# Merging score jobs, pairing output evacuations and moving a weight load in a fused attention + MLP kernel

## The chip, the cores and the metric

The kernel runs on one core of one Trainium2 chip. The metric is the device time of one execution in microseconds. Profiles give a span that is some 2 us shorter than the timed execution.

## The reference

```python
def _attn_ref(q, k, v):                     # batch 8, heads 8, seq 576, head_dim 64, fp32
    scores = q @ k.transpose(0, 1, 3, 2) / np.sqrt(64)
    mask_local   = (rel >= 0) & (rel < 32)                              # heads 0..3
    mask_strided = (rel >= 0) & (pos[None, :] % 32 == pos[:, None] % 32)  # heads 4..7
    attn = softmax(where(mask, scores, -1e9))
    return attn @ v

def _moe_ref(x, w_in, w_out):               # x: 4608 tokens x 512, d_ff 2048
    h = x @ w_in
    return (h * tanh(softplus(h))) @ w_out  # mish
```

The kernel computes only the scores that the masks keep. A local head is 6 windows of 96 queries. A strided head is, per residue mod 8, a product of 72 by 72.

## The kernel before

The main loop goes over 9 blocks of 512 tokens. In block t, TensorE does the first MLP product (8 groups, each evacuated by a Mish on ScalarE) with the transposes of q and k of batch t+1 woven in, and then the second product (16 groups, output rows `ot` 0 to 3) with the attention of batch t+1 woven in by steps. Blocks 7 and 8 have no attention left. I call the two parts of a block its first and second half, and what comes before block 0 the prologue.

A score job is a few matmuls into one PSUM tile, one exp on ScalarE, and one multiplication with a mask on VectorE or GpSimd:

```python
def qk(self, kind, hp, hf, meng, from_mm=False):     # 8 jobs per batch
    ps = tile_s(from_mm); pt = P[self.n % NP]        # NP = 8 buffers of [128, 2, 352]
    ...                                              # 6 or 8 small matmuls
    nc.scalar.activation(pt[0:n, :, 0:288], ps[0:n, :, 0:288], AF.Exp, scale=scale)
    meng.tensor_tensor(out=pt[0:n, :, 0:288], in0=pt[0:n, :, 0:288], in1=<mask>, op=ALU.mult)
```

`pv(kind, i)` multiplies with v (four matmuls), then VectorE takes a reciprocal and a product. `xt(kind, hf)` transposes the result, and ScalarE copies it to `xT`, the input of the MLP. The output is copied out row by row of a two-row PSUM tile:

```python
p = po[ot // 2]                                      # [128, 2, 512] fp32: two banks
for fc in range(4 * g4, 4 * g4 + 4):
    nc.tensor.matmul(p[:, ot % 2, :], lhsT=gT[...], rhs=w_out[:, fc, :], ...)
if g4 == 3:
    osb = o_pool.tile([128, DM], F32, ...)
    nc.scalar.copy(osb[:], p[:, ot % 2, :])
    nc.sync.dma_start(out[r:r + 128, :], osb[:])
```

The steps of the attention beside the 16 groups, and the prologue's GpSimd order:

```python
[Q("s",0,0,Po)], [], [Q("s",1,0,Dv)], [Q("s",0,1,Po)], [Q("s",1,1,Dv), V("s",0)],
[Q("l",0,0,Po), V, V], [Q("l",1,0,Po), V], [Q("l",0,1,Po), V, V], [Q("l",1,1,Dv), V],
... [V("l",5)], [X("l",1)]

cast_qk_loc(0, Po, Dv)
load_w_in()                       # GpSimd queue, cast fp32 -> bf16 by the transfer
a.qk("s", 0, 0, Po) ...           # strided jobs, masks half on GpSimd
cast(Sc, vs ...)                  # on ScalarE
cast(Po, vl ...) x2               # on GpSimd: waits for v
...
a.qk("l", ..., Po) x4             # local masks all on GpSimd
load_qk_str(1); load w_out        # GpSimd queue
cast_qk_loc(1, Po, Po); cast_v(1, Po, Po); load_qk_str(2) ...
```

The softmax here doesn't subtract the row's maximum and nothing guards it: scores larger than these inputs give would overflow.

Of the kernel before, what the change touches and what calls it, by code (L numbers as in the profile page):

```python
# [10 lines left out]
F32 = mybir.dt.float32  # L11
BF16 = mybir.dt.bfloat16
AF = mybir.ActivationFunctionType
# [3 lines left out]
NW = 6  # L17
WQ = 96
CL, PL = 6, 96
CS, PN = 8, 72  # L20
# [3 lines left out]
def _masks():  # L24
    kk = np.arange(128)[:, None]
    qq = np.arange(WQ)[None, :]
    rel = qq + 32 - kk
    band = (rel >= 0) & (rel < STRIDE)
    loc = np.stack([band & (kk >= 32)] + [band] * (NW - 1), axis=1).astype(np.float32)
    p = np.arange(PN)  # L30
    st = ((p[:, None] % 4 == p[None, :] % 4) & (p[:, None] <= p[None, :])).astype(np.float32)
    stm = np.zeros((128, 4, PN), np.float32)
    stm[:PN] = st[:, None, :]
    bf = ml_dtypes.bfloat16
    return loc.astype(bf), stm.astype(bf)


@with_exitstack
def kernel(ctx, tc, q, k, v, moe_w_in, moe_w_out, out):
    nc = tc.nc  # L40
    B, H, S, D = q.shape
    DM, DF = moe_w_in.shape
    NT = B * S
    assert S == 576 and D == 64 and H == 8 and DM == 512 and DF == 2048
    scale = 1.0 / float(np.sqrt(D))
# [10 lines left out]
    const = ctx.enter_context(tc.tile_pool(name="const", bufs=1))  # L56
    w_in = const.tile([128, 4, DF], BF16, name="w_in")
    w_out = const.tile([128, 16, DM], BF16, name="w_out")
    xT = const.tile([128, 4, RT], BF16, name="xT")
    loc = const.tile([128, NW, WQ], BF16, name="loc")  # L60
    stm = const.tile([128, 4, PN], BF16, name="stm")
    ident = const.tile([128, 128], BF16, name="ident_sb")
    vl32 = const.tile([128, NW, 4, D], F32, name="vl32")
    vs32 = const.tile([128, 4, CS, D], F32, name="vs32")
# [9 lines left out]
    kTl = const.tile([128, 2, 32 + S], BF16, name="kTl")  # L74
    qTs = const.tile([128, 4 * 4 * PN], BF16, name="qTs")
    kTs = const.tile([128, 4 * 4 * PN + 64], BF16, name="kTs")
    NP = 8
    P = [const.tile([128, 2, 352], BF16, name=f"P{i}") for i in range(NP)]
    gate = const.tile([1, 256], BF16, name="gate")
    x_l = const.tile([128, NW, 256], BF16, name="x_l")  # L80
    x_s = const.tile([128, CS, 256], BF16, name="x_s")

    g_pool = ctx.enter_context(tc.tile_pool(name="gp", bufs=2))
    small = ctx.enter_context(tc.tile_pool(name="small", bufs=4))
    o_pool = ctx.enter_context(tc.tile_pool(name="op", bufs=3))
    PS = bass.MemoryType.PSUM
    ps_mm = ctx.enter_context(tc.tile_pool(name="psmm", bufs=2, space=PS))
    ps_s = ctx.enter_context(tc.tile_pool(name="pss", bufs=1, space=PS))
# [30 lines left out]
                v[b, 0:4, WQ * i - 32:WQ * i + WQ, :].rearrange("h p d -> p h d"),  # L119
            )  # L120

    def load_w_in():
        for c in range(4):
            nc.gpsimd.dma_start(
                w_in[:, :, 512 * c:512 * c + 512],
                moe_w_in.rearrange("(cc p) f -> p cc f", p=128)[:, :, 512 * c:512 * c + 512],
            )

    def cast(eng, out_, in_):
        if eng is nc.scalar:  # L130
            nc.scalar.copy(out_, in_)  # L131
        else:
            eng.tensor_copy(out_, in_)  # L133
# [41 lines left out]
    def t_steps(b):  # L175
        return [lambda a=a: t_step(b, *a) for a in T_ORDER]

    class Attn:
        def __init__(self, b):
            self.b = b  # L180
            self.P = {}
            self.n = 0

        def qk(self, kind, hp, hf, meng, from_mm=False):
            ps = tile_s(from_mm)
            pt = P[self.n % NP]
            self.n += 1
            self.P[kind, hp, hf] = pt
            if kind == "l":
                for w in range(3):  # L190
                    i = 3 * hf + w
                    for e in range(2):
                        nc.tensor.matmul(  # L193
                            ps[:, e, WQ * w:WQ * w + WQ],
                            lhsT=kTl[64 * e:64 * e + 64, hp, WQ * i:WQ * i + 128],
                            rhs=qTl[64 * e:64 * e + 64, hp, WQ * i:WQ * i + WQ],
                            start=True, stop=True,
                        )
                n, mk = 128, loc[:, 3 * hf:3 * hf + 3, :]
            else:  # L200
                for u in range(4):
                    c0 = PN * (4 * (2 * hp + u // 2) + 2 * hf + u % 2)
                    for e in range(2):
                        nc.tensor.matmul(  # L204
                            ps[:, e, PN * u:PN * u + PN],
                            lhsT=kTs[64 * e:64 * e + 64, c0:c0 + 128],
                            rhs=qTs[64 * e:64 * e + 64, c0:c0 + PN],
                            start=True, stop=True,
                        )
                n, mk = PN, stm[0:PN]  # L210
            nc.scalar.activation(pt[0:n, :, 0:288], ps[0:n, :, 0:288], AF.Exp, scale=scale)  # L211
            meng.tensor_tensor(  # L212
                out=pt[0:n, :, 0:288], in0=pt[0:n, :, 0:288],
                in1=mk.rearrange("p w c -> p (w c)").unsqueeze(1).to_broadcast([n, 2, 288]),
                op=ALU.mult,
            )

        def pv(self, kind, i):
            po = tile_t("po")[:, 0:4 * (D + 1)].rearrange("p (h d) -> p h d", h=4)
            for h in range(4):  # L220
                if kind == "l":
                    hf, w = divmod(i, 3)
                    pt = self.P["l", h // 2, hf][:, h % 2]
                    n, m, c0, rhs = 128, WQ, WQ * w, vl[self.b % 2][:, i, h, :]
                else:
                    pt = self.P["s", h // 2, i // 4][:, i % 2]
                    n, m, c0 = PN, PN, PN * (2 * (h % 2) + i // 2 % 2)
                    rhs = vs[self.b % 2][0:PN, h, i, :]
                nc.tensor.matmul(  # L229
                    po[:, h, :], lhsT=pt[0:n, c0:c0 + 128], rhs=rhs,  # L230
                    start=True, stop=True,
                )
            dst = (x_l if kind == "l" else x_s)[0:m, i, :]
            rden = small.tile([128, 4], F32, tag="rden", name="rden")
            nc.vector.reciprocal(rden[0:m, :], po[0:m, :, D])  # L235
            nc.vector.tensor_tensor(  # L236
                out=dst.rearrange("p (h d) -> p h d", h=4), in0=po[0:m, :, 0:D],
                in1=rden[0:m, :].unsqueeze(2).to_broadcast([m, 4, D]), op=ALU.mult,
            )
# [28 lines left out]
    def attn_steps(b):  # L268
        a = Attn(b)
        Po, Dv = nc.gpsimd, nc.vector  # L270
        Q = lambda kd, hp, hf, e: (lambda: a.qk(kd, hp, hf, e))
        V = lambda kd, i: (lambda: a.pv(kd, i))
        X = lambda kd, hf: (lambda: a.xt(kd, hf))
        return [
            [Q("s", 0, 0, Po)], [], [Q("s", 1, 0, Dv)], [Q("s", 0, 1, Po)],
            [Q("s", 1, 1, Dv), V("s", 0)], [Q("l", 0, 0, Po), V("s", 1), V("s", 2)],
            [Q("l", 1, 0, Po), V("s", 3)], [Q("l", 0, 1, Po), V("s", 4), V("s", 5)],
            [Q("l", 1, 1, Dv), V("s", 6)], [V("s", 7)], [X("s", 0), V("l", 0)],
            [X("s", 1), V("l", 1)], [V("l", 2)], [V("l", 3), V("l", 4), X("l", 0)],
            [V("l", 5)], [X("l", 1)],  # L280
        ]


# [24 lines left out]
    def mlp2(t, gT, fc_major=False):  # L308
        po = {}

        def group(ot, g4):
            if ot // 2 not in po:
                po[ot // 2] = ps_mm.tile([128, 2, 512], F32, tag="mm", name="pso")
            p = po[ot // 2]
            for fc in range(4 * g4, 4 * g4 + 4):
                nc.tensor.matmul(  # L316
                    p[:, ot % 2, :], lhsT=gT[:, fc, 128 * ot:128 * ot + 128], rhs=w_out[:, fc, :],
                    start=(fc == 0), stop=(fc == 15),
                )
            if g4 == 3:  # L320
                osb = o_pool.tile([128, DM], F32, tag="osb", name="osb")
                nc.scalar.copy(osb[:], p[:, ot % 2, :])  # L322
                r = 512 * t + 128 * ot
                nc.sync.dma_start(out[r:r + 128, :], osb[:])
        order = [(ot, g4) for ot in range(4) for g4 in range(4)]
        if fc_major:
            order = [(ot, g4) for g4 in range(4) for ot in range(4)]
        return [lambda o=o: group(*o) for o in order]


    with tc.manual_schedule():
# [11 lines left out]
        for i in range(2):  # L343
            Dv.memset(vs[i][:, :, :, D:D + 1], 1.0)
            Dv.memset(vl[i][:, :, :, D:D + 1], 1.0)
        for i in range(NP):
            Dv.memset(P[i][:], 0.0)

        a = Attn(0)
        t_step(0, "s", "k", 0, Dv)  # L350
# [1 line left out]
        t_step(0, "s", "q", 0, Sc)  # L352
        t_step(0, "s", "q", 1, Sc)
        cast_qk_loc(0, Po, Dv)
        load_w_in()
        a.qk("s", 0, 0, Po)
        a.qk("s", 1, 0, Dv, True)
        a.qk("s", 0, 1, Po, True)
        a.qk("s", 1, 1, Dv)
        cast(Sc, vs[0][0:PN, :, :, 0:D], vs32[0:PN])  # L360
        for i in range(0, NW, 3):
            cast(Po, vl[0][:, i:i + 3, :, 0:D], vl32[:, i:i + 3, :, :])
        for hp in range(2):
            t_step(0, "l", "k", hp, Dv)
            t_step(0, "l", "q", hp, Sc)
        a.qk("l", 0, 0, Po, True)
        a.qk("l", 1, 0, Po, True)
        a.qk("l", 0, 1, Po)
        a.qk("l", 1, 1, Po, True)
        for j in range(8):  # L370
            a.pv("s", j)
        nc.sync.dma_start(gate[:], x_s[0:1, 5, :])
# [77 lines left out]
```

## Time and profile before

The median is 379.0 us (377.88 to 379.56). Cut at the first MLP matmul of each block and at the last matmul, at the times which the chain view gives, the profile's span of 378.9 us is this:

| part | us |
|---|---|
| prologue, to the first MLP matmul | 40.15 |
| block 0 | 45.8 |
| blocks 1 to 6 | 230.5 |
| blocks 7 and 8 | 58.8 |
| tail, after the last matmul | 3.6 |

In the views below, PE is TensorE, ACT ScalarE, DVE VectorE, POOL GpSimd. A line of the waits reads "engine, line waited for who: us in total, times, longest". A line of the chain reads "start, us, what". A line of the timeline reads "start, us, engine, line, operation, out<-in, shapes, count, and the idle time before with what ended it". The lines themselves are in the prediction.

### The profile page before, as it was taken

How to read it: one execution, taken by the hardware profiler on the slowest of the kernel's cores; microseconds unless marked ns; L12 is line 12 of the kernel's file. 1: busy time of each engine (PE TensorE's matmuls, PEld its weight loads, DVE VectorE, ACT ScalarE, POOL GpSimd, SP SyncE). 2: the span in 40 equal slices, each digit the busy share in tenths (PEclk: the TensorE clock that was granted, in tenths of full speed). 3: DMA queues.
4: the chain of work that ended last, by engine and by line, in shares of the span. 5: the costliest groups of instructions: out<-in, count | busy, mean ns of one | idle time of the engine just before them, and what ended most of it. 6: DMA issues, size and time to landing. Idle time of an engine off the chain costs nothing.

```text
span 378.9 us, 6623 instructions
## 1 busy us (share of the span) xinstructions
PE 328.1 (87%) x2784; PEld 172.6 (46%) x2784; DVE 118.3 (31%) x323; ACT 178.0 (47%) x225; POOL 118.0 (31%) x107
## 2 busy tenths in 40 slices
PE   0453999779988898889999989998999899999995
PEld 0332454344544454445457944554455444444442
DVE  3552023631335133513352335233523352000000
ACT  1631455236553555355645564556455645613521
POOL 4408832911058004901391129102910230000000
PEclk9999999989999999999999999999999999999999
DMA  7999999329901790169114941390100010011002
GB/s 187 207 188 219 194 266 205 59 85 215 145 29 55 193 164 31 57 159 188 40 57 110 198 81 57 98 196 31 57 28 2 29 56 29 0 55 57 0 33 78
DMA packets 49421, 39.21 MB, mean 104 GB/s; under 512 B 27376, under 2 KB 42480, under 8 KB 49392
## 3 DMA queue, kind: packets, MB, share of 16 engines
q1 hardware_dynamic: 38768, 29.88, 34.0%
q0 software_dynamic: 10624, 8.92, 15.0%
q8 instruction: 21, 0.34, 0.4%
q14 instruction: 8, 0.07, 0.1%
HBM read 38.26 MB, written 9.44 MB: 126 GB/s over the span
## 4 chain that ended last, share of the span: by engine, by line
PE 75%; ACT 7%; DVE 5%; SPq 4%; issue 4%; DMA 3%; POOL 1%; ACTq 0%; POOLq 0%
PE psh L301 34%; PE pso L316 29%; SPq L117 4%; ACT osb L322 3%; PE po L229 3%; DMA vl<-in_v_dram 3%; ACT P L211 3%; PE tr L153 2%; PE tr L162 2%; DVE P L212 2%; PE ps L204 2%; PE ps L193 1%; DVE x_l L236 1%; PE trx L249 1%; PE trx L259 1%
## 5 line engine op out<-in xcount | busy, mean ns | idle before, releaser
L316 PE MATMUL pso<-w_out,gT 128*128 128x512 bf16 x576 | 143.2, 381 | 8.8 <-ACT osb L322 8.8
L301 PE MATMUL psh<-xT,w_in 128*128 128x512 bf16 (+1 forms) x640 | 135.6, 362 | 3.7 <-ACT xT L131 3.7
L305 ACT ACTIVATE gT<-psh 128x1024 bf16<-128x1024 f32 x72 | 73.7, 1023 | 61.0 <-PE psh L301 61.0
L301 PEld LDWEIGHTS <-w_in 128*128 128x128 bf16 x640 | 60.1, 99 | 57.1 <-issue 7.1
L316 PEld LDWEIGHTS <-gT 128*128 128x128 bf16 x576 | 50.1, 98 | 55.4 <-issue 11.7
L211 ACT ACTIVATE P<-ps 72x576 bf16<-72x576 f32 (+1 forms) x64 | 41.0, 649 | 26.9 <-PE ps L193 18.1
L212 POOL TENSOR_TENSOR P<-P,stm 72x576 bf16<-72x576 bf16 x16 | 20.4, 1280 | 102.1 <-ACT P L211 102.1
L131 ACT COPY xT<-trx 128x576 bf16<-128x576 bf16 x32 | 20.4, 641 | 50.4 <-PE trx L259 30.7
L322 ACT COPY osb<-pso 128x512 f32<-128x512 f32 x36 | 21.1, 585 | 43.7 <-PE pso L316 43.7
L212 POOL TENSOR_TENSOR P<-P,loc 128x576 bf16<-128x576 bf16 x25 | 31.7, 1272 | 16.6 <-ACT P L211 16.5
L229 PEld LDWEIGHTS <-P 72*128 72x128 bf16 (+1 forms) x448 | 22.8, 102 | 23.4 <-POOL P L212 7.7
L235 DVE RECIPROCAL rden<-po 72x4 f32<-72x4 f32 (+1 forms) x112 | 19.5, 174 | 44.1 <-PE po L229 44.1
L236 DVE TENSOR_TENSOR x_s<-po,rden 72x256 bf16<-72x256 f32 x64 | 26.9, 421 | 2.2
L212 DVE TENSOR_TENSOR P<-P,stm 72x576 bf16<-72x576 bf16 x16 | 9.9, 618 | 42.4 <-ACT P L211 42.4
L133 DVE COPY kTs<-tr 128x576 bf16<-128x576 bf16 x16 | 7.3, 458 | 47.0 <-PE tr L153 46.9
L229 PE MATMUL po<-vl,P 128*128 128x65 bf16 x192 | 13.7, 202 | 8.4 <-POOL P L212 7.4
L229 PE MATMUL po<-vs,P 72*128 72x65 bf16 x256 | 18.3, 201 | 3.0 <-DVE x_s L236 2.4
L102 POOL DMA_DIRECT2D ks<-in_k_dram x8 | 6.3, 783 | 46.8 <-PE tr L153 45.9
L236 DVE TENSOR_TENSOR x_l<-po,rden 96x256 bf16<-96x256 f32 x48 | 20.2, 421 | 1.7
L133 DVE COPY kTl<-tr 128x576 bf16<-128x576 bf16 x16 | 12.1, 757 | 19.5 <-PE tr L162 19.5
L133 POOL CAST vl<-vl 128x768 bf16<-128x768 f32 x16 | 12.9, 826 | 15.0 <-DMA vl<-in_v_dram 15.0
L133 DVE COPY qTl<-tr 128x576 bf16<-128x576 bf16 x14 | 10.6, 756 | 14.8 <-PE tr L162 14.8
(41 smaller groups left out, 204.5 us busy)
## 6 DMA issues: line engine op xcount, KB each, us to landing
out_dram<-osb SPq DMA_DIRECT2D x36, 256.0 KB, 2.0
vl<-in_v_dram SPq DMA_DIRECT2D x40, 128.0 KB, 10.6
kl<-in_k_dram SPq DMA_DIRECT2D x8, 576.0 KB, 8.3
ql<-in_q_dram SPq DMA_DIRECT2D x8, 576.0 KB, 8.0
vs<-in_v_dram SPq DMA_DIRECT2D x8, 576.0 KB
ks<-in_k_dram POOLq DMA_DIRECT2D x8, 288.0 KB, 9.3
qs<-in_q_dram POOLq DMA_DIRECT2D x8, 288.0 KB, 9.9
w_in<-in_moe_w_in_dram POOLq DMA_DIRECT2D x4, 512.0 KB, 14.6
```

What stands on the lines that cost most here:

```text
L117: nc.sync.dma_start(vl32[:, i, :, :], v[b, 0:4, WQ * i - 32:WQ * i + WQ, :].rearrange("h p d -> p h d"),)
L131: nc.scalar.copy(out_, in_)
L133: eng.tensor_copy(out_, in_)
L211: nc.scalar.activation(pt[0:n, :, 0:288], ps[0:n, :, 0:288], AF.Exp, scale=scale)
L212: meng.tensor_tensor(out=pt[0:n, :, 0:288], in0=pt[0:n, :, 0:288], in1=mk.rearrange("p w c -> p (w c)").unsqueeze(1).to_broadcast([n, 2, 2 ...
L229: nc.tensor.matmul(po[:, h, :], lhsT=pt[0:n, c0:c0 + 128], rhs=rhs, start=True, stop=True,)
L235: nc.vector.reciprocal(rden[0:m, :], po[0:m, :, D])
L236: nc.vector.tensor_tensor(out=dst.rearrange("p (h d) -> p h d", h=4), in0=po[0:m, :, 0:D], in1=rden[0:m, :].unsqueeze(2).to_broadcast([m, ...
L301: nc.tensor.matmul(ps[:, u, o:o + n], lhsT=w_in[:, cc, fc * 128:(fc + 1) * 128], rhs=xT[:, cc, a:a + n], start=(cc == 0), stop=(cc == 3),)
L305: nc.scalar.activation(gT[:, 2 * g:2 * g + 2, :], ps[:], AF.Mish)
L316: nc.tensor.matmul(p[:, ot % 2, :], lhsT=gT[:, fc, 128 * ot:128 * ot + 128], rhs=w_out[:, fc, :], start=(fc == 0), stop=(fc == 15),)
L322: nc.scalar.copy(osb[:], p[:, ot % 2, :])
```

## The change

The change has three intents. Score jobs go from eight to six per batch and are ordered by tokens instead of by heads, so that the first P·V products can start after one job. The output is evacuated in pairs, so that no copy stands between two rows of a tile. w_in is issued behind the v loads of batch 0, so that v lands first. With the jobs, the step order changes (the last transposes move from step 15 to 14), the prologue's masks all move to VectorE, and the cast of vs in the prologue moves from ScalarE to GpSimd. The mask tiles shrink to one window, which the masking operation repeats.

```diff
-    NP = 8
-    P = [const.tile([128, 2, 352], BF16, name=f"P{i}") for i in range(NP)]
+    P_s = [const.tile([PN, 2, 6 * PN + 56], BF16, name=f"Ps{i}") for i in range(3)]
+    P_l = [const.tile([128, 2, 4 * WQ + 32], BF16, name=f"Pl{i}") for i in range(3)]
...
+    S_UNITS = [(jj, h) for jj in range(4) for h in range(4)]
+    S_JOBS = [S_UNITS[0:6], S_UNITS[6:12], S_UNITS[12:16]]
...
-            nc.scalar.activation(pt[0:n, :, 0:288], ps[0:n, :, 0:288], AF.Exp, scale=scale)
+            nw = nu * w                                # 432, 432, 288 strided; 384 local
+            nc.scalar.activation(pt[0:n, :, 0:nw], ps[0:n, :, 0:nw], AF.Exp, scale=scale)
...
+            [Q("s", 0, Dv)], [], [Q("s", 1, Dv)], [Q("s", 2, Po), V("s", 0)],
+            [Q("l", 0, Po), V("s", 1)], [Q("l", 1, Po), V("s", 2), V("s", 3)],
+            [Q("l", 2, Dv), V("s", 4)], [V("s", 5), V("s", 6)], ...
+            [X("l", 1)], [],
...
-            if g4 == 3:
-                osb = o_pool.tile([128, DM], F32, tag="osb", name="osb")
-                nc.scalar.copy(osb[:], p[:, ot % 2, :])
+            if g4 == 3 and ot % 2 == 1:
+                osb = o_pool.tile([128, 2, DM], F32, tag="osb", name="osb")
+                nc.scalar.copy(osb[:], p[:])
...
         cast_qk_loc(0, Po, Dv)
-        load_w_in()
-        a.qk("s", 0, 0, Po) ... four strided jobs, Po and Dv
-        cast(Sc, vs[0][0:PN, :, :, 0:D], vs32[0:PN])
+        cast(Po, vs[0][0:PN, :, :, 0:D], vs32[0:PN])
+        load_w_in(0, 2)
+        a.qk("s", 0, Dv); a.qk("s", 1, Dv, True); a.qk("s", 2, Dv, True)
         for i in range(0, NW, 3):
             cast(Po, vl[0][:, i:i + 3, :, 0:D], vl32[:, i:i + 3, :, :])
+        load_w_in(2, 4)
...
-        a.qk("l", 0, 0, Po, True) ... four local jobs, Po
+        a.qk("l", 0, Dv); a.qk("l", 1, Dv, True); a.qk("l", 2, Dv, True)
```

More of the change, by code (lines that the diff above doesn't have):

```diff
@@ L28, in _masks @@
     band = (rel >= 0) & (rel < STRIDE)
-    loc = np.stack([band & (kk >= 32)] + [band] * (NW - 1), axis=1).astype(np.float32)
     p = np.arange(PN)
-    st = ((p[:, None] % 4 == p[None, :] % 4) & (p[:, None] <= p[None, :])).astype(np.float32)
-    stm = np.zeros((128, 4, PN), np.float32)
-    stm[:PN] = st[:, None, :]
+    st = (p[:, None] % 4 == p[None, :] % 4) & (p[:, None] <= p[None, :])
     bf = ml_dtypes.bfloat16
-    return loc.astype(bf), stm.astype(bf)
+    return band.astype(np.float32).astype(bf), st.astype(np.float32).astype(bf)
 @with_exitstack
@@ L59 @@
     xT = const.tile([128, 4, RT], BF16, name="xT")
-    loc = const.tile([128, NW, WQ], BF16, name="loc")
-    stm = const.tile([128, 4, PN], BF16, name="stm")
+    loc = const.tile([128, WQ], BF16, name="loc")
+    stm = const.tile([PN, PN], BF16, name="stm")
     ident = const.tile([128, 128], BF16, name="ident_sb")
@@ L84 @@
     small = ctx.enter_context(tc.tile_pool(name="small", bufs=4))
-    o_pool = ctx.enter_context(tc.tile_pool(name="op", bufs=3))
+    o_pool = ctx.enter_context(tc.tile_pool(name="op", bufs=2))
     PS = bass.MemoryType.PSUM
@@ L120, in load_v, with load_w_in @@
             )
-    def load_w_in():
-        for c in range(4):
+    def load_w_in(c0, c1):
+        for c in range(c0, c1):
             nc.gpsimd.dma_start(
@@ L176, in t_steps @@
         return [lambda a=a: t_step(b, *a) for a in T_ORDER]
+    S_UNITS = [(jj, h) for jj in range(4) for h in range(4)]
+    S_JOBS = [S_UNITS[0:6], S_UNITS[6:12], S_UNITS[12:16]]
+    S_AT = {u: (i, n) for i, job in enumerate(S_JOBS) for n, u in enumerate(job)}
     class Attn:
@@ L180, in __init__, with qk @@
             self.b = b
-            self.P = {}
-            self.n = 0
-        def qk(self, kind, hp, hf, meng, from_mm=False):
+        def qk(self, kind, i, meng, from_mm=False):
             ps = tile_s(from_mm)
-            pt = P[self.n % NP]
-            self.n += 1
-            self.P[kind, hp, hf] = pt
             if kind == "l":
-                for w in range(3):
-                    i = 3 * hf + w
+                nu, n, w, pt, mk = 4, 128, WQ, P_l[i], loc
+                for u in range(nu):
+                    hp, c0 = u // 2, WQ * (2 * i + u % 2)
                     for e in range(2):
                         nc.tensor.matmul(
-                            ps[:, e, WQ * w:WQ * w + WQ],
-                            lhsT=kTl[64 * e:64 * e + 64, hp, WQ * i:WQ * i + 128],
-                            rhs=qTl[64 * e:64 * e + 64, hp, WQ * i:WQ * i + WQ],
+                            ps[:, e, WQ * u:WQ * u + WQ],
+                            lhsT=kTl[64 * e:64 * e + 64, hp, c0:c0 + 128],
+                            rhs=qTl[64 * e:64 * e + 64, hp, c0:c0 + WQ],
                             start=True, stop=True,
                         )
-                n, mk = 128, loc[:, 3 * hf:3 * hf + 3, :]
             else:
-                for u in range(4):
-                    c0 = PN * (4 * (2 * hp + u // 2) + 2 * hf + u % 2)
+                nu, n, w, pt, mk = len(S_JOBS[i]), PN, PN, P_s[i], stm
+                for u, (jj, h) in enumerate(S_JOBS[i]):
+                    c0 = PN * (4 * h + jj)
                     for e in range(2):
@@ L209, in qk @@
                         )
-                n, mk = PN, stm[0:PN]
-            nc.scalar.activation(pt[0:n, :, 0:288], ps[0:n, :, 0:288], AF.Exp, scale=scale)
+            nw = nu * w
+            nc.scalar.activation(pt[0:n, :, 0:nw], ps[0:n, :, 0:nw], AF.Exp, scale=scale)
+            pm = pt[0:n, :, 0:nw].rearrange("p e (u c) -> p e u c", u=nu)
             meng.tensor_tensor(
-                out=pt[0:n, :, 0:288], in0=pt[0:n, :, 0:288],
-                in1=mk.rearrange("p w c -> p (w c)").unsqueeze(1).to_broadcast([n, 2, 288]),
+                out=pm, in0=pm,
+                in1=mk[0:n, :].unsqueeze(1).unsqueeze(1).to_broadcast([n, 2, nu, w]),
                 op=ALU.mult,
@@ L221, in pv @@
                 if kind == "l":
-                    hf, w = divmod(i, 3)
-                    pt = self.P["l", h // 2, hf][:, h % 2]
-                    n, m, c0, rhs = 128, WQ, WQ * w, vl[self.b % 2][:, i, h, :]
-                else:
-                    pt = self.P["s", h // 2, i // 4][:, i % 2]
-                    n, m, c0 = PN, PN, PN * (2 * (h % 2) + i // 2 % 2)
-                    rhs = vs[self.b % 2][0:PN, h, i, :]
+                    n, m, rhs = 128, WQ, vl[self.b % 2][:, i, h, :]
+                    pt, c0 = P_l[i // 2][:, h % 2], WQ * (2 * (h // 2) + i % 2)
+                else:
+                    n, m, rhs = PN, PN, vs[self.b % 2][0:PN, h, i, :]
+                    job, u = S_AT[i // 2, h]
+                    pt, c0 = P_s[job][:, i % 2], PN * u
                 nc.tensor.matmul(
@@ L270, in attn_steps @@
         Po, Dv = nc.gpsimd, nc.vector
-        Q = lambda kd, hp, hf, e: (lambda: a.qk(kd, hp, hf, e))
+        Q = lambda kd, i, e: (lambda: a.qk(kd, i, e))
         V = lambda kd, i: (lambda: a.pv(kd, i))
@@ L274, in attn_steps @@
         return [
-            [Q("s", 0, 0, Po)], [], [Q("s", 1, 0, Dv)], [Q("s", 0, 1, Po)],
-            [Q("s", 1, 1, Dv), V("s", 0)], [Q("l", 0, 0, Po), V("s", 1), V("s", 2)],
-            [Q("l", 1, 0, Po), V("s", 3)], [Q("l", 0, 1, Po), V("s", 4), V("s", 5)],
-            [Q("l", 1, 1, Dv), V("s", 6)], [V("s", 7)], [X("s", 0), V("l", 0)],
-            [X("s", 1), V("l", 1)], [V("l", 2)], [V("l", 3), V("l", 4), X("l", 0)],
-            [V("l", 5)], [X("l", 1)],
+            [Q("s", 0, Dv)], [], [Q("s", 1, Dv)],
+            [Q("s", 2, Po), V("s", 0)],
+            [Q("l", 0, Po), V("s", 1)],
+            [Q("l", 1, Po), V("s", 2), V("s", 3)],
+            [Q("l", 2, Dv), V("s", 4)], [V("s", 5), V("s", 6)],
+            [V("s", 7), V("l", 0)], [V("l", 1)], [X("s", 0), V("l", 2)],
+            [X("s", 1), V("l", 3)], [X("l", 0), V("l", 4)], [V("l", 5)],
+            [X("l", 1)], [],
         ]
@@ L319, in group @@
                 )
-            if g4 == 3:
-                osb = o_pool.tile([128, DM], F32, tag="osb", name="osb")
-                nc.scalar.copy(osb[:], p[:, ot % 2, :])
-                r = 512 * t + 128 * ot
-                nc.sync.dma_start(out[r:r + 128, :], osb[:])
+            r = 512 * t + 256 * (ot // 2)
+            if g4 == 3 and ot % 2 == 1:
+                osb = o_pool.tile([128, 2, DM], F32, tag="osb", name="osb")
+                nc.scalar.copy(osb[:], p[:])
+                nc.sync.dma_start(out[r:r + 256, :].rearrange("(o p) d -> p o d", o=2), osb[:])
         order = [(ot, g4) for ot in range(4) for g4 in range(4)]
@@ L345 @@
             Dv.memset(vl[i][:, :, :, D:D + 1], 1.0)
-        for i in range(NP):
-            Dv.memset(P[i][:], 0.0)
+        for i in range(2):
+            Dv.memset(vl[i][0:32, 0, :, D:D + 1], 0.0)
+        for p in P_s + P_l:
+            Dv.memset(p[:], 0.0)
         a = Attn(0)
@@ L354 @@
         cast_qk_loc(0, Po, Dv)
-        load_w_in()
-        a.qk("s", 0, 0, Po)
-        a.qk("s", 1, 0, Dv, True)
-        a.qk("s", 0, 1, Po, True)
-        a.qk("s", 1, 1, Dv)
-        cast(Sc, vs[0][0:PN, :, :, 0:D], vs32[0:PN])
+        cast(Po, vs[0][0:PN, :, :, 0:D], vs32[0:PN])
+        load_w_in(0, 2)
+        a.qk("s", 0, Dv)
+        a.qk("s", 1, Dv, True)
+        a.qk("s", 2, Dv, True)
         for i in range(0, NW, 3):
             cast(Po, vl[0][:, i:i + 3, :, 0:D], vl32[:, i:i + 3, :, :])
+        load_w_in(2, 4)
         for hp in range(2):
@@ L365 @@
             t_step(0, "l", "q", hp, Sc)
-        a.qk("l", 0, 0, Po, True)
-        a.qk("l", 1, 0, Po, True)
-        a.qk("l", 0, 1, Po)
-        a.qk("l", 1, 1, Po, True)
+        a.qk("l", 0, Dv)
+        a.qk("l", 1, Dv, True)
+        a.qk("l", 2, Dv, True)
         for j in range(8):
```

## The prediction

> **What bounds the kernel now.** I read four views in turn: the page's slices, the chain that ended last, the waits, and timelines of single stretches. The slices first (a digit is busy time in tenths of 1/40 of the span, 9.5 us):
>
> ```profile
> PE   0453999779988898889999989998999899999995
> DVE  3552023631335133513352335233523352000000
> POOL 4408832911058004901391129102910230000000
> DMA  7999999329901790169114941390100010011002
> ```
>
> TensorE (PE) is the bound from the fifth slice on, with dents. Before it, the DMA engines are full for 66 us and PE is mostly idle. The chain by line says the same: 62.6% matmuls of the two MLP lines, the rest mostly small waits. The chain in the prologue:
>
> ```profile
> 17.98 12.10 DMA vl<-in_v_dram
> ...
> 31.01 2.51 POOL P L212 x2
> ...
> 40.15 1.86 PE psh L301 x4
> ```
>
> So the v rows of batch 0 land at 30.1 us; GpSimd, stuck in order at their cast, starts the local masks only at 31.0; the first MLP matmul starts at 40.15. The waits on PE inside the loop:
>
> ```profile
> PE pso L316 <- ACT osb L322: 8.8, 18, 0.7
> PE psh L301 <- ACT xT L131: 3.7, 4, 1.0
> ```
>
> 18 waits are two in each of 9 blocks of 512 tokens: after output rows ot=0 and ot=2, PE waits for the copy of that half before it may write the other half of the same tile. In the last two blocks, with no attention beside them, it is plain:
>
> ```profile
> 330.30 3.47 PE pso L316 x16
> 333.77 0.03 ACTq L322
> 333.80 0.04 issue
> 333.83 0.59 ACT osb L322
> 334.43 0.04 issue
> 334.47 7.08 PE pso L316 x32
> ```
>
> 3.47 us for 16 matmuls is 216 ns each; the gap is 0.70 us; afterwards 32 matmuls run through the change of tile with no gap. Last, one VectorE mask in block 0 of 2.99 us, against 0.48 us in the others:
>
> ```profile
> 69.56 1.27 POOL L212 TENSOR_TENSOR P<-P,loc 128x576 bf16<-128x576 bf16 x1
> 70.77 1.46 POOL L133 CAST kl<-kl 96x1536 bf16<-96x1536 f32 x1
> 72.18 1.46 POOL L133 CAST ql<-ql 96x1536 bf16<-96x1536 f32 x1
> 73.59 2.12 POOL L133 CAST vs<-vs 72x2048 bf16<-72x2048 f32 x1
> ```
>
> The mask asked at 70.96, just after the kl cast began, and ended at 73.95.
>
> **What the Trainium skill says.** "ScalarE: Activation LUTs", What ACT_TABLE_LOAD costs: about 1283 ns a load, and an activation with immediates takes 186 ns + 0.833 ns a column. The trace agrees: 1283 ns mean; 649 ns for 576 columns, 1023 ns for 1024 (the formula gives 666 and 1039). "SBUF — State Buffer", SBUF: two separate sides: a VectorE operation with two SBUF inputs and a GpSimd operation hold a shared port pair exclusively, the loser blocks. The 2.99 us agrees. "PSUM — Partial Sum Buffer", PSUM bank collisions: only accesses to the same bank collide. Here PE waits on a copy of the other bank, so that wait is the program's tracking of the whole tile, not the chip's need. "DMA: Bandwidth & Descriptors", Issuing engines are not separate DMA queues: all transfers share 16 engines and interleave. The trace agrees: w_in issued at 8.4 us on one queue and v on the other both stretch to about 30 us.
>
> **The change, part by part.** I have the old total as a sum: start of the MLP 40.15; first half of block 0 18.15, second half 27.7; first halves of blocks 1–6 95.8 together; second halves 23.05 in blocks 1–2 and 22.1 in 3–6, 134.5; blocks 7 and 8 29.4 each; tail 3.6. Sum 378.7 against a span of 378.9.
>
> *Evacuation in pairs.* One copy of 1024 columns instead of two of 512: 585 − 427 = 158 ns fixed, so 1.01 us for 1.17. ScalarE's saving is nothing; what counts is that no copy comes between halves of a tile. Blocks 7 and 8 have 29.4 − 2 × 13.82 (64 matmuls of 216 ns) = 1.75 us of gap and refill each, all of it gone: −3.5. The next block's second group takes the last copied tile; its first group runs 1.73 us, longer than 1.01, so no wait takes its place. But the very last copy is 0.43 us longer, and its transfer has 512 KB where 256 KB took 2.0 us; at the 214 to 280 GB/s of the slices that is about 0.9 us more. Tail +1.3.
>
> *Six jobs and the new step order.* Score matmuls stay 56 per batch. Exp: from 8 × 0.65 = 5.2 us to 2 × 0.89 + 0.65 + 3 × 0.81 = 4.9 us, so little; the first job after the table load is 0.24 us longer, and PE's stall there (0.33 us: 1.28 + 0.65 against two groups of 0.86) grows to about 0.6. GpSimd masks fall from five to three per batch: at 2.2 ns a column 6.4 us become 1.28 + 2 × 1.68 = 4.6; VectorE goes from about 1.5 to 0.6 + 0.6 + 0.55. In old second halves the gaps on PE's chain (blocks 3–6) are: table load 0.33, two copies 0.70 each, waits for x of 0.4 and 0.7, five refills of about 0.15 after them; 22.1 − these leaves about 18.5, which is also the sum 13.8 + 2.0 scores + 1.8 for 14 PV + 1.0 transposes. I walked the new order by hand with these durations. Left are the table load 0.6, one or two stalls around steps 8 and 9 of about 0.5 each (eight PV need 0.62 us each on VectorE, and the last local mask falls between them), refills 0.3, a few small ones: 20.1 with VectorE's port free, 20.7 with the mask waiting for GpSimd's. I take 20.7. The last transposes move one step ahead, so their copy to xT ends beside the last group, and the 1.0 us at the start of blocks 1–3 goes too. Blocks 1–6: 134.5 → 124.2, −10.3. Block 0: no 2.99 us mask, no copies between, no 1.25 us at its end: 27.7 → 21, −6.7.
>
> *w_in behind v.* Without w_in, what must land by the end of v is about 3.2 MB (q and k 1.7, constants 0.1, v 1.3); at the slices' 250 KB/us from 3 us on, that is 16 to 17 us instead of 30. GpSimd then casts v early. The local PV no longer wait 6.5 us; the chain becomes: qs lands at 12, scores and masks to 17, local transposes to 19.5, three exps of 0.81 and masks to 22.9, eight PV at 0.57 to 27.5, three more to 29.2, and from the third local PV's end to the first MLP matmul 4.5 us as before (35.7 to 40.15). That is 33.7; with one or two masks blocked by the v casts I take 34: −6.15. w_in's first half should land by about 24 and the second by 30, before use. First-half time of block 0 is kept; its first matmuls ran at half rate (four in 1.86 us) and will again.
>
> Sum: −6.15 − 6.7 − 10.3 − 3.5 + 1.3 = −25.4, so 379.0 − 25.4 = 353.6 us.
>
> **Rivals.** (1) VectorE meets GpSimd at the last local mask: my walk has it asking 0.6 us before GpSimd's last mask ends and the casts begin. In blocks 1–5 of the old trace it came in just that way and won (0.48 us), in block 0 it came 0.2 us after the cast began and lost 2.5 us. If it loses in blocks 0–5, 6 × 2.5 = 15 us come back: about 368. (2) DMA is the bound up to 66 us anyway: bytes are only reordered, and a block 0 that starts 6 us earlier finds k, q or v of batch 1, or w_out, not landed. For: full slices. Against: w_out and k, q of batch 1 are now issued by GpSimd at about 20 us instead of 36 to 40, and by my count 8.6 MB can land by 43 us where 7.1 are needed. If true, 3 to 6 us of the prologue's gain come back: 357 to 360. (3) The copies were hidden anyway: excluded by blocks 7 and 8. (4) A four-dimensional mask with a repeated pattern runs slower on VectorE (1 element a cycle, 1.05 for 0.6 us): about +0.5 per block, 357.
>
> **Range and chances.** Sum 353.6. Everything lucky (20.1 per half, start at 32.5) gives 348 or a little below; rival 1 or 2 in part gives 360. Range 346 to 364. Faster by over 2% means below 371.4; only rivals 1 and 2 together get there: 0.96. Within 2% 0.03, slower 0.01.
>
> **What would show it.** Right: no wait of pso for osb among PE's waits; none of psh for xT except at block 0; first MLP matmul near 34; v landed before 20; blocks 1–6 at about 36.7 us each; block 0 at 39; the osb copy 1.01 us. Wrong: masks on VectorE above 2 us while GpSimd casts (rival 1); PE waits for transfers between 34 and 70 us (rival 2); VectorE masks near 1.05 us (rival 4); the first MLP matmul still near 40, if v's landing is not set by w_in but by how its own small rows are issued.

## The result

The changed kernel takes 356.65 us (356.35 to 356.86, 4 runs) against 378.44 us in the same rounds. A ratio here and below is the mean time of one kernel's fast runs over the mean of the other's fast runs of the same rounds, so not quite the ratio of the medians quoted: 0.942, with an interval of 0.939 to 0.945. By parts of the profile:

| part | before | predicted | after |
|---|---|---|---|
| prologue | 40.15 | 34 | 37.23 |
| block 0, first half | 18.15 | 18.15 | 17.75 |
| block 0, second half | 27.7 | 21 | 20.35 |
| blocks 1 to 6 | 230.5 | 220.0 | 218.9 |
| blocks 7 and 8 | 58.8 | 55.3 | 55.5 |
| tail | 3.6 | 4.9 | 5.0 |

The slices of the changed kernel, of 8.9 us each:

```profile
PE   0537999899989998999899989998999989999994
DVE  3478025632363236323642364235613460000000
POOL 3290236911091109310841065005600400000000
DMA  7999999969611991099109901870110011011012
```

PE's dents have shrunk to one slice in about four, one per block, that still reads 8; the DMA engines are still full to about 70 us. Among the waits of PE there is none of `pso` for `osb` any more, and one of `psh` for `xT`, at block 0. The longest that is left in the loop is a new one:

```profile
PE po L227 <- DVE rden L233: 9.3, 9, 1.3
```

Seven of these nine waits, 1.2 us each, are one in each of blocks 0 to 6: PE's next P·V product waits for VectorE, which works off its reciprocals late, behind its last local mask. They are the dents. The chain of the last block answers to the one shown of before:

```profile
321.99 13.81 PE psh L301 x64
335.81 13.83 PE pso L316 x64
```

All 64 matmuls of the second product run without a gap in 13.83 us, where before two gaps of 0.70 us stood in 15.6 us. The timeline of ScalarE at the start of block 2's second half shows something that I had not predicted:

```profile
127.50 1.02 ACT L305 ACTIVATE gT<-psh 128x1024 bf16<-128x1024 f32 x1 [0.96 <-PE psh L301]
128.54 1.28 ACT L209 ACT_TABLE_LOAD   x1
129.84 0.89 ACT L209 ACTIVATE Ps<-ps 72x864 bf16<-72x864 f32 x1
131.18 0.89 ACT L209 ACTIVATE Ps<-ps 72x864 bf16<-72x864 f32 x1 [0.46 <-PE ps L202]
```

The table load starts right behind the last Mish, while PE still works at the scores. In the kernel before it waited for them (a wait of L211 for L204, seven times, 3.0 us in total). So the first exp, though longer, ends in time, and the stall of PE there is about 0.05 us instead of the 0.6 predicted.

The prologue is where the prediction was furthest off. First VectorE, then GpSimd, in the prologue of the changed kernel:

```profile
15.64 5.52 DVE L211 TENSOR_TENSOR Ps<-Ps,stm 72x864 bf16<-72x864 bf16 x3 [3.11 <-ACT Ps L209]
21.08 1.41 DVE L130 COPY kTl<-tr 128x576 bf16<-128x576 bf16 x2
```

```profile
15.49 1.90 POOL L130 CAST vs<-vs 72x2048 bf16<-72x2048 f32 x1 [7.20 <-DMA vs<-in_v_dram]
17.33 1.53 POOL L121 DMA_DIRECT2D w_in<-in_moe_w_in_dram  x2
18.84 2.01 POOL L130 CAST vl<-vl 128x768 bf16<-128x768 f32 x2
```

Three masks that take 0.60, 0.60 and about 0.45 us when VectorE is alone took 5.52 us, and they lie beside the casts of v and the two issues of w_in between these casts. The copies of the local k, behind them in VectorE's order, came at 21.1, where the prediction had the masks done at 17.

### The profile page after: what moved, and what is told of

It reads as the page before. It is cut to its first block, busy times and chain, and to the rows that moved or that the text cites. A ratio compares the mean times of both kernels' runs of the same rounds, so it can differ in the third digit from the quotient of the medians.

```text
span 354.6 us, 6492 instructions
## 1 busy us (share of the span) xinstructions
PE 318.3 (90%) x2784; PEld 171.2 (48%) x2784; DVE 124.9 (35%) x327; ACT 173.6 (49%) x190; POOL 100.6 (28%) x88
## 4 chain that ended last, share of the span: by engine, by line
PE 79%; DVE 8%; ACT 6%; DMA 3%; issue 3%; POOL 0%; ACTq 0%; POOLq 0%
PE psh L301 36%; PE pso L316 29%; PE po L227 4%; DMA qs<-in_q_dram 3%; PE tr L150 2%; PE tr L159 2%; ACT Pl L209 2%; DVE Pl L211 2%; PE ps L191 2%; ACT Ps L209 2%; DVE x_s L234 2%; PE ps L202 2%; DVE Ps L211 1%; DVE qTl L130 1%; PE trx L257 1%
## 5 line engine op out<-in xcount | busy, mean ns | idle before, releaser
L301 PEld LDWEIGHTS <-w_in 128*128 128x128 bf16 x640 | 60.3, 99 | 55.3 <-issue 3.4
L211 POOL TENSOR_TENSOR Ps<-Ps,stm 72x576 bf16<-72x576 bf16 x7 | 8.9, 1269 | 101.4 <-ACT Ps L209 101.4
L323 ACT COPY osb<-pso 128x1024 f32<-128x1024 f32 x18 | 18.2, 1012 | 27.8 <-PE pso L316 27.8
L227 PE MATMUL po<-vs,Ps 72*128 72x65 bf16 x256 | 18.2, 201 | 11.8 <-DVE rden L233 8.7
L209 ACT ACTIVATE Pl<-ps 128x768 bf16<-128x768 f32 x24 | 19.2, 811 | 13.8 <-PE ps L191 13.8
L211 POOL TENSOR_TENSOR Pl<-Pl,loc 128x768 bf16<-128x768 bf16 x14 | 22.6, 1639 | 1.9 <-ACT Pl L209 1.9
L209 ACT ACTIVATE Ps<-ps 72x864 bf16<-72x864 f32 (+1 forms) x24 | 19.1, 806 | 7.1 <-PE ps L202 7.0
L211 DVE TENSOR_TENSOR Ps<-Ps,stm 72x864 bf16<-72x864 bf16 (+1 forms) x17 | 14.0, 831 | 23.5 <-ACT Ps L209 23.5
L227 PEld LDWEIGHTS <-Ps 72*128 72x128 bf16 x256 | 12.6, 101 | 18.9 <-issue 9.4
L130 POOL CAST kl<-kl 96x1536 bf16<-96x1536 f32 x8 | 13.7, 1707 | 17.3 <-DMA kl<-in_k_dram 17.3
L130 POOL CAST vs<-vs 72x2048 bf16<-72x2048 f32 x8 | 15.1, 1893 | 10.5 <-DMA vs<-in_v_dram 10.5
```

Of the source, the lines that this page charges most:

```text
L130: eng.tensor_copy(out_, in_)
L209: nc.scalar.activation(pt[0:n, :, 0:nw], ps[0:n, :, 0:nw], AF.Exp, scale=scale)
L211: meng.tensor_tensor(out=pm, in0=pm, in1=mk[0:n, :].unsqueeze(1).unsqueeze(1).to_broadcast([n, 2, nu, w]), op=ALU.mult,)
L227: nc.tensor.matmul(po[:, h, :], lhsT=pt[0:n, c0:c0 + 128], rhs=rhs, start=True, stop=True,)
L301: nc.tensor.matmul(ps[:, u, o:o + n], lhsT=w_in[:, cc, fc * 128:(fc + 1) * 128], rhs=xT[:, cc, a:a + n], start=(cc == 0), stop=(cc == 3),)
L323: nc.scalar.copy(osb[:], p[:])
```

## The experiments

Twelve kernels ran, all correct. Their times, with the ratio to the kernel before of the same rounds:

| run | median us | ratio | first MLP matmul | block 0 |
|---|---|---|---|---|
| changed kernel | 356.65 | 0.942 | 37.23 | 38.1 |
| pair_only | 373.69 | 0.983 | 39.78 | 44.7 |
| halves | 364.84 | 0.959 | | |
| two_copies | 356.68 | 0.940 | 37.26 | 38.9 |
| xt_late | 361.67 | 0.953 | 36.42 | 39.7 |
| w_in_early | 365.05 | 0.960 | 34.67 | 48.8 |
| w_in_late_only | 380.25 | 0.998 | 33.47 | 51.5 |
| port | 357.29 | 0.939 | | |
| port_l2pool | 356.85 | 0.941 | 33.64 | 41.9 |
| port_w_out | 360.46 | 0.950 | 34.04 | 45.9 |
| best | 357.92 | 0.944 | 33.69 | 47.3 |
| w_in_early_vl | 354.26 | 0.931 | 34.91 | 38.1 |
| best_vl | 352.56 | 0.925 | 33.36 | 39.1 |

A stage's time is that of the one execution that was profiled, which for port_w_out (361.04 us) and best (360.74 us) was one of the slower ones. The profiles of halves and port fell on runs that were slow (369.88 and 364.33 us against 364.25 to 365.23 and 356.6 to 357.77). I leave their stages out and use only their fast times. How far a prologue scatters by itself shows in xt_late, whose prologue is that of the changed kernel: there VectorE's first mask began 0.15 us ahead of the cast of vs instead of 0.15 us behind it, was done in 0.60 us, and the first MLP matmul came 0.8 us sooner. In the profiles of the fast runs of the other kernels, blocks 1 to 6 take 218.8 to 218.9 us wherever the changed kernel's main loop stands unchanged: what distinguishes these runs lies in the prologue, block 0 and the tail.

### The pairs: which part of the gain, and why

**pair_only** puts the pair evacuation alone into the kernel before.

> The kernel before with the pair evacuation alone. My sum: blocks 7 and 8 lose 1.75 us each, the tail grows by 1.3, blocks 0 to 6 lose two waits of 0.7 each, and the starts of blocks 1 to 3 get 0.4 longer, since the copy ahead of the last xT copy is now 1.01 instead of 0.59: 378.4 - 3.5 + 1.3 - 9.8 + 1.2 = 367.6 us. Rival, that beside attention other waits take the place of the two copies: only blocks 7 and 8 gain, about 377.5 us.

Measured: 373.69 us, ratio 0.983 with an interval of 0.976 to 0.990, some 6.5 us faster, though at the threshold of 2% the verdict is unclear. That is between the two. The 18 waits for `osb` are gone, but others came: PE's wait of `psh` for `xT` grew from 3.7 to 5.0 us (longest 1.4, as expected), and this stretch of the chain in block 2 shows one more:

```profile
149.71 0.03 ACTq L323
149.74 0.04 issue
149.78 0.21 ACT osb L323
149.99 0.07 issue
150.07 0.61 issue
150.69 0.67 ACT P L211
151.35 0.04 issue
151.39 0.32 PE ps L193 x6
```

In the old step order the pair's copy of 1.01 us starts just ahead of a local job's exp; the exp comes some 0.7 us late, and the next scores, which use the same PSUM tile, wait for it (six times, 1.5 us in all). The new order has no score job left when the first pair is done.

**halves** undoes the pairs in the changed kernel.

> The changed kernel with the pair evacuation undone (a copy and a transfer for each half, as before). If the terms add, it loses 3.5 in blocks 7 and 8, 1.4 in each of blocks 0 to 6, and gets 1.3 back at the tail: 356.6 + 12.0 = 368.6 us. Rival, that the new step order would hide the copies: 359 us. PE's waits for osb come back as 18 in either case; their total tells (near 9 us, or near 4).

Measured: 364.84 us, ratio 0.959 against 0.942. By the ratios that is some 6 us worse, by the medians 8. My 12 was too much: beside attention the two copies cost less than their 1.4 us a block. The 18 waits are back, with 6.6 us in total (in the profile of the slow run).

**two_copies** evacuates at the new moment, but with two copies of 512 columns.

```diff
-                nc.scalar.copy(osb[:], p[:])
+                nc.scalar.copy(osb[:, 0], p[:, 0, :])
+                nc.scalar.copy(osb[:, 1], p[:, 1, :])
```

> The changed kernel with each pair evacuated at the same moment but by two copies of 512 columns, one behind the other. Theory: what the pair bought is that no copy stands between the halves of a tile; the number of copies is nothing beside it: 18 x (2 x 0.585 - 1.01) = 2.9 us more on ScalarE, none of it on PE's path except 0.15 us at the tail, and no wait of pso for osb: 356.8 us, ratio to the kernel before within 0.3% of the changed kernel's 0.942. Rival, that ScalarE's time counts: 359 us or more.

Measured: 356.68 us, ratio 0.940: as the changed kernel. No wait for `osb` returns. So the gain is in when the copy stands, not in how many copies there are, and the extra time on ScalarE costs nothing here.

**xt_late** moves the last transposes back to step 15.

> The changed kernel with the last transposes of x moved back from step 14 to step 15. Theory: the copy to xT then stands behind the pair's copy of 1.01 us on ScalarE, and PE waits 1.4 us at the starts of blocks 1, 2 and 3, which need those rows, and of no other: 356.6 + 4.3 = 360.9 us. Rival, that the wait is hidden by something else: 356.6 us.

Measured: 361.67 us, 5.0 us more than the changed kernel's median, and the waits say where:

```profile
PE psh L301 <- ACT xT L128: 5.0, 4, 1.4
```

In the changed kernel this line has 0.7 us, once. The three others are the starts of blocks 1 to 3, 1.4 us each, as worked out. So moving one step is worth 4 to 5 us once the pair's copy exists (4.2 by the ratios).

### The prologue: w_in or the masks

**w_in_early** issues all of w_in at its old place in the changed kernel.

```diff
         cast_qk_loc(0, Po, Dv)
+        load_w_in(0, 4)
         cast(Po, vs[0][0:PN, :, :, 0:D], vs32[0:PN])
-        load_w_in(0, 2)
...
-        load_w_in(2, 4)
```

> The changed kernel with all of w_in issued at its old place, behind the kl cast. Theory: the v rows land near 30 us again and the first MLP matmul moves from 37.2 to about 38.5, so 358 us: most of what the later w_in gave was eaten in the changed kernel by VectorE masks blocked behind GpSimd casts, so undoing it costs little. Rival, that the 2.9 us which the prologue gained are all due to w_in: first matmul at 40, 359.5 us or more.

Measured: 365.05 us, and both theories fall. The first MLP matmul came not later but earlier, at 34.67, although the second half of vl was cast only at 29.1: with the local masks on VectorE, nothing but the last P·V products needs that half, and they stand at 31. What the later w_in did in the prologue was to put more GpSimd work beside VectorE's masks. But block 0 took 48.8 us instead of 38.1. The timelines of VectorE and of GpSimd there:

```profile
62.42 9.52 DVE L211 TENSOR_TENSOR Pl<-Pl,loc 128x768 bf16<-128x768 bf16 x1 [0.93 <-ACT Pl L209]
```

```profile
58.69 0.83 POOL L130 CAST vl<-vl 128x768 bf16<-128x768 f32 x1 [8.16 <-DMA vl<-in_v_dram]
...
62.42 1.28 POOL L211 TENSOR_TENSOR Ps<-Ps,stm 72x576 bf16<-72x576 bf16 x1
63.65 3.22 POOL L211 TENSOR_TENSOR Pl<-Pl,loc 128x768 bf16<-128x768 bf16 x2
66.82 1.45 POOL L130 CAST kl<-kl 96x1536 bf16<-96x1536 f32 x1
68.23 1.46 POOL L130 CAST ql<-ql 96x1536 bf16<-96x1536 f32 x1
69.64 1.89 POOL L130 CAST vs<-vs 72x2048 bf16<-72x2048 f32 x1
```

This is my first rival, in a form that I had not thought of. GpSimd waits in order for v of batch 1 (58.7 us), issues four transfers, and only then starts block 0's masks, just as VectorE asks for its last one. From there GpSimd works without a gap, and VectorE's mask ends at 71.94, 0.41 us after the last of these six instructions (69.64 + 1.89 = 71.53). PE waits 9.9 us here, once, against 1.2 us in the changed kernel. That is 8.7 of the 10.7 us that block 0 lost. The other 2 are slower matmuls: the granted clock in this profile is 0.5 from about 66 to 76 us, the matmuls of the second product, when PE goes on at 72.6 us, follow each other after 427 ns instead of 215, and PE is busy for 38.9 us of block 0 instead of 36.9.

The new theory: a shorter prologue is given back in block 0, because GpSimd's order is tied to a transfer that does not come sooner.

**w_in_late_only** moves w_in behind the vl casts in the kernel before, and nothing else.

> The kernel before with w_in behind the vl casts and nothing else. Theory: there the local masks are GpSimd's, which waits for v in order, so here the order counts: v lands near 18 us, first matmul at 34 instead of 40.15. If block 0 keeps its 45.8 us, 380 - 6 = 374 us. Rival, that block 0 takes it back since GpSimd comes late to its masks there: block 0 49 us or more, 377 to 380 us.

Measured: 380.25 us, ratio 0.998. The rival was right. The first matmul came at 33.47, 6.7 us sooner, and block 0 took 51.5 us instead of 45.8, again with GpSimd waiting for v of batch 1, which it cast at 59.8 instead of 49.1. By itself this part of the change is worth nothing.

### Removing the lock in the prologue, and in block 0

**port** keeps GpSimd away from VectorE's masks in the prologue.

```diff
-        cast(Po, vs[0][0:PN, :, :, 0:D], vs32[0:PN])
-        load_w_in(0, 2)
...
-        a.qk("s", 2, Dv, True)
+        a.qk("s", 2, Po, True)
         for i in range(0, NW, 3): cast(Po, vl[0] ...)
-        load_w_in(2, 4)
+        load_w_in(0, 4)
         for hp in range(2):
             t_step(0, "l", "k", hp, Dv)
             t_step(0, "l", "q", hp, Sc)
+            if hp == 0: cast(Sc, vs[0][0:PN, :, :, 0:D], vs32[0:PN])
```

> The changed kernel with GpSimd kept off VectorE's masks in the prologue: the cast of vs goes to ScalarE (between two transposes that wait anyway), the third strided mask goes to GpSimd ahead of the vl casts, and w_in is issued behind the vl casts. Theory, shared port: the strided masks take 0.6 us each instead of 5.5 in sum, and the first MLP matmul comes at about 34 instead of 37.2: 353.3 us. Rival, that vs simply lands later than I thought (15.5 instead of 12.5) and sets the chain: no gain, 356.5 us.

Measured: 357.29 us; the fast runs have 356.6 to 357.77, so by the total no gain. Taken alone this would have spoken for the rival. The three runs below have the same prologue, fast profiles, and their first MLP matmul at 33.6 to 34.0: the 3.2 to 3.6 us are gained there, and VectorE's two strided masks take 0.60 us each. So GpSimd's work beside the masks was the cause of the late ones; port moves the cast of vs, one mask and w_in at once, and does not tell them apart. The gain is lost again later.

**port_l2pool** gives the last local mask of block 0 to GpSimd too, so that VectorE has nothing to be locked out of.

```diff
-            [Q("l", 2, Dv), V("s", 4)], ...
+            [Q("l", 2, Po if b == 1 else Dv), V("s", 4)], ...
```

> The port run with one mask moved: the last local mask of block 0 goes to GpSimd instead of VectorE. In port the first MLP matmul came at 33.4, yet block 0 took 49.8 us instead of 38.1, with that mask 10.5 us long on VectorE. Theory, shared port: GpSimd comes late to its masks because it waits in order for v of batch 1 (58.8 us), then works without a gap, and VectorE is locked out; without a VectorE mask there no run is near 364 us, and block 0 is 41 us or less: 353 to 356 us. Rival, that PE waits in block 0 for the transfers themselves: block 0 stays near 50 us and 364 us occurs again.

Measured: 356.85 us (356.6 to 358.41), no run near 364, but not the 353 to 356 expected either. Block 0 is 41.9 us, a little over the 41 expected, with one wait of PE for GpSimd's strided mask, 2.8 us: that is GpSimd's lateness alone. The 49.8 and 10.5 us of the expectation are read from port's slow run. Against port's fast runs nothing is gained, so these lost little to the lock; and one slow run of four there against none of four here does not show that the lock made it slow.

**port_w_out** tries to make v of batch 1 land sooner by issuing w_out later.

```diff
-        load_qk_str(1); w_out (4 transfers); cast_qk_loc(1); cast_v(1)
+        load_qk_str(1); cast_qk_loc(1); w_out 0,1; cast vs(1); w_out 2,3; cast vl(1)
```

> The port run with the transfers of w_out moved behind the casts of k and q (first half) and of vs (second half) of batch 1. Theory: v of batch 1 lands at about 50 us instead of 58.8, GpSimd is free before block 0's masks begin, VectorE's last local mask there takes under 1 us, and block 0 takes 38.1 as in the changed kernel: first matmul 33.4, total 352.8 us. Rival, that the transfers up to v of batch 1 take until about 58 us in whatever order: block 0 stays at 42 to 50 us and the total at 356.7 or 364. Failure of another kind: PE waits for w_out from 52 us on.

Measured: 360.46 us: a miss. The last of v of batch 1 was cast at 57.3 instead of the 59.7 of port_l2pool, VectorE's mask took 6.69 us, block 0 45.9. The rival holds: in both orders that were tried, the transfers up to there fill the DMA engines until about 57 us.

**best** adds the split tail to that run: the last two output rows get a PSUM tile, a copy and a transfer each.

> As the run with w_out moved, and the last two output rows of the last block get a PSUM tile each, a copy of 512 columns each and a transfer of 256 KB each. Theory: the tail is 3.6 us again instead of 5.0, and no wait comes into block 8, since the two halves are different tiles: 1.3 us less than the run before it, 351.5 us. Rival, that the tail is set by the transfer's latency alone: no gain, 352.8 us.

Measured: 357.92 us, with runs from 356.14 to 360.74. The scatter is too wide to read 1.2 us from the total. From the profiles it can be read: from the start of block 7 to the end of the span it is 59.1 us, against 60.4 in port_w_out and in the changed kernel. VectorE's mask in block 0 took 8.24 us.

**best_vl** leaves the transfers alone and takes the wait out of GpSimd's order instead. The vl casts of batch 1 go behind block 0's three GpSimd masks, the issues of the next k and q go ahead, and the tail is split; the rest is port's.

```diff
         cast_qk_loc(1, Po, Po)
-        cast_v(1, Po, Po)
+        cast(Po, vs[1][0:PN, :, :, 0:D], vs32[0:PN])
         load_qk_str(2); load_qk_loc(2)
-        load_v(2)
...
+            if t == 0: at[5].append(vl_1)      # vl casts of batch 1, then load_v(2)
```

> The port run, with GpSimd no longer waiting for v of batch 1 ahead of block 0's masks: the two casts of vl for batch 1 stand behind its three masks, the transfers that followed them stand before; and the last block's two last rows are evacuated apart. Theory: the transfers still end near 57 us, but nothing waits for them in order: first matmul 33.6, VectorE's last local mask under 2 us, block 0 38.1 to 39.5 us, tail 1.2 less than in the changed kernel: 352.5 us, and no run near 364. Rival, that PE now waits for the casts or for the transfers themselves: block 0 41 us or more, 355 us or more.

Measured: 352.56 us (351.72 to 352.82), ratio 0.925 with an interval of 0.922 to 0.928. First matmul 33.36, block 0 39.1, tail 3.7. VectorE's last local mask, and GpSimd beside it:

```profile
61.84 0.82 DVE L211 TENSOR_TENSOR Pl<-Pl,loc 128x768 bf16<-128x768 bf16 x1 [0.93 <-ACT Pl L209]
```

```profile
57.55 1.27 POOL L211 TENSOR_TENSOR Ps<-Ps,stm 72x576 bf16<-72x576 bf16 x1 [6.24 <-ACT Ps L209]
59.02 3.23 POOL L211 TENSOR_TENSOR Pl<-Pl,loc 128x768 bf16<-128x768 bf16 x2 [0.21 <-ACT Pl L209]
62.20 1.16 POOL L130 CAST vl<-vl 128x768 bf16<-128x768 f32 x1
65.66 0.83 POOL L130 CAST vl<-vl 128x768 bf16<-128x768 f32 x1 [2.31 <-DMA vl<-in_v_dram]
```

GpSimd now waits for the scores, as it should, and has its masks done in time. VectorE waits for one mask of GpSimd, not for six instructions. PE waits 1.2 us for a vl cast, once. This version beats both kernels. Its split tail also shows what PE's old wait for `osb` was. In the last block ScalarE copies row ot=2 from 343.44 to 344.02 us, while PE writes row ot=3, which now is another tile, and PE does not stop:

```profile
333.00 13.83 PE pso L318 x64
```

**w_in_early_vl** does the same to the changed kernel with w_in at its old place, without the port edits and the split tail.

> The changed kernel with w_in at its old place, and with the casts of vl for batch 1 behind block 0's masks, as in the run before. Theory: the later w_in bought the changed kernel nothing in the prologue, the local masks' move to VectorE did: first matmul 34.7 although v lands near 30; and with GpSimd free in time the lock of 9.5 us in block 0 is gone, block 0 39 us: 355 us, a little faster than the changed kernel. Rival, that w_in must come behind v for block 0's sake: block 0 44 us or more, 360 us or more.

Measured: 354.26 us, ratio 0.931, with block 0 at 38.1 and the first matmul at 34.91. So once GpSimd is free in time, w_in ahead of v is no worse than behind it: this kernel is faster than the changed one.

## Why the prediction was right, and where it was not

The total was 353.6 with a range of 346 to 364, and 356.65 came. The parts add up: −2.9 in the prologue, −0.4 and −7.35 in block 0, −11.6 in blocks 1 to 6, −3.3 in blocks 7 and 8, +1.3 at the tail make −24.3 of the span, for the −25.4 predicted. The timed median fell by only 21.8: the profile of the kernel before is of an execution of 381.16 us, 2.7 over the median beside which the changed kernel was timed. So most of the 3 us by which the total missed is not an error of the parts. In the parts themselves, a prologue 3.2 us too slow was offset for the greater part by blocks 0 to 6, which came out 2.2 us faster than predicted.

- **Pairs: right.** Blocks 7 and 8 and the tail came within 0.2 us of the sum. That PE's wait was the program's tracking of the tile and not a collision of banks is shown by the split tail: the copy of one bank while PE writes another holds up nothing once the two are different tiles. What I priced wrong was the value of the copies beside attention (1.4 us a block in my expectations); halves and pair_only show 0.6 to 0.9.
- **Six jobs and the new order: right, and a little better.** Blocks 1 to 6 gave 11.6 us for 10.3. The term "PE's stall there (0.33 us) grows to about 0.6" is wrong: it is 0.05, because the table load no longer waits for the scores. Why the compiled program places that wait differently I have not tested. Against the gain there stands PE's wait for VectorE at the last local mask, 1.2 us a block, where the prediction had one or two stalls of about 0.5 each; the two errors offset each other in part. The move of the transposes by one step is confirmed by xt_late.
- **Block 0: right.** 20.35 us for the 21 predicted, with VectorE's mask at 0.83 instead of 2.99.
- **w_in behind v: the step that failed.** I put −6.15 us on it, and the prologue gave −2.9. The mis-sized term is "with one or two masks blocked by the v casts I take 34": the three strided masks took 5.52 us for the 1.65 that they need, 3.9 us of blocking where I had allowed 0.3. The landing was right: the casts of vl start at 18.84 and wait for no transfer. The attribution was wrong as well. The run with w_in at its old place has its first matmul at 34.67, so the rest of the change brings 5.5 us to the prologue, and w_in's move takes 2.6 us of it away. The traces say that the local masks on VectorE are what does it (they start at 21.9 us, where GpSimd's started at 31.0), but no run moved them alone. What the move gave the changed kernel was in block 0. There GpSimd had v of batch 1 cast by 56.3 us instead of 59.5, and VectorE asked 0.4 us before GpSimd's last mask ended and went next. The prediction had not worked this out for block 0; that it came out well there was luck.
- **Rival 1** did not occur in the changed kernel (its last local mask took 0.83 to 0.89 us in every block), but it decided three of the experiments (w_in_early, port_w_out, best), where that mask took 6.7 to 9.5 us. The form was not "six blocks of 2.5 us" but one block, when GpSimd is late. The lines in the prediction already held a hint: the mask of 2.99 us ended at 73.95, after two casts of GpSimd (to 73.64) and not after one. **Rival 2** was half right: PE never waited for a transfer in block 0, but the transfers set when GpSimd could start. **Rival 3** was rightly excluded, **rival 4** did not occur: the masks of 864 columns take 0.60 us.

Still open: why two of the four fast runs of best are some 3 us slower than the others (their mean granted clock is 0.984 and 0.989 against 0.995, as in runs with a long wait of PE in block 0, but only the slowest has a profile), and which rule decides who gets the port at a change of hands. The slow runs of port and halves may have the same cause as w_in_early; as only slow runs were profiled there, that is not shown.

## What to carry to other kernels

A gain before a stage is only kept if every engine that the next stage needs is free sooner as well: look for an engine that waits in order for a transfer and has work behind that wait which others need soon. Between VectorE and GpSimd, count not busy time but who stands beside whom: a mask of 0.6 us became 9.5 us. And a copy costs what it stands in front of: the same copies, moved by one output row, went from 18 waits to none.

## What the Trainium skill lacked or had wrong

- "ScalarE: Activation LUTs", What ACT_TABLE_LOAD costs, gives 1283 ns for the load and 1380 ns of drain, 2.66 us for every switch. The load's 1283 ns agree. No drain is seen here: Mish ends at 128.52, the load runs from 128.54 to 129.82, and the exp starts at 129.84. The switch cost 1.32 us.
- "SBUF — State Buffer", SBUF: two separate sides, says that the one which starts first holds the port pair for the whole instruction and the other blocks. It does not say that the loser may lose several times in a row: one VectorE mask, which asked at 62.42 just as the first of them began, waited through GpSimd's three masks and three casts and took 9.52 us. In blocks 1 to 5 of the changed kernel it waited for one mask and then went ahead of the next cast (0.89 us).
- No page that I read puts the two together: GpSimd executes in order, so a cast that waits for a transfer delays the masks behind it and moves them beside VectorE's. Block 0 took 41.9 us where only the lateness counted (port_l2pool), 45.9 to 48.8 where the lock came on top (port_w_out, best, w_in_early), and 38.1 to 39.1 with neither.
